# Block sums in small steps, a fast product begun one chunk later, and reloads on another queue

## The chip, the cores and the metric

The kernel runs on one core of one Trainium2 chip. Its metric is the device time of one execution in microseconds (us). Three runs took 912.3, 912.48 and 913.36 us; the median is 912.48 us. The profiled execution took 912.57 us, and 910.5 us of it lie between its first and its last instruction (the span).

## What is computed

Three stages follow one another: an attention over blocks, a gated feed-forward stage, and a second feed-forward stage with a residual. Only the last one is touched. Cut to what matters:

```
def _moe2_ref(x, g_ln, w_ch1, w_ch2):          # x: 4 x 576 x 512
    mu, var = mean(x), mean((x - mu) ** 2)      # over the last axis
    xn = (x - mu) / sqrt(var + 1e-06) * g_ln
    ch = maximum(xn @ w_ch1, 0.0) @ w_ch2       # w_ch1 512 x 2048, w_ch2 2048 x 512
    return x + ch
```

The weights arrive as 64-bit floats. Each is turned into a 32-bit float on the chip and then cut into a high and a low part, so that a product of two numbers is three matrix multiplications (high by high, low by high, high by low).

## The kernel before, in words

**Tiling.** The 2304 tokens are four groups of 512 (0, 1, 2, 3) and one of 256 (group 4, called `Z` in the code). The hidden dimension of 2048 is cut into eight chunks of 256 (`NC2` = 8, chunks 0 to 7). For each chunk every group goes through the first product (`em_c1`, 24 matmuls of 512 columns, written to PSUM tiles `ph`, five buffers), a ReLU on ScalarE and a split into high and low on VectorE (`h`), and then the second product (`em_c2`, six matmuls for each tile of 128 tokens, PSUM tiles `po`, three buffers), which VectorE adds to `acc` (line 794). The second product of a group is issued after the first product of the next group.

**The fast form.** For a pair of groups (`PAIRS`: 0 with 3, and 2 with 1) the first product can be made with seven block products in place of eight (`em_c1s`, 42 matmuls for the pair in place of 48). It needs four sums of blocks of the weights (`forms` inside `chunk_jobs`, tiles `ta` and `tb`) and four sums of blocks of the inputs (tiles `SF`, in the trace `s`). `sum_forms` makes the input sums: VectorE and GpSimd (POOL) add and subtract, ScalarE writes the high part of a sum, POOL the low part. Both pairs share the four `SF` tiles, so each sum is also stored to memory (`s_scr`) and reloaded (`load_form`, 1 MB each) whenever the other pair is next. `S3`, the fourth `SF` tile, holds half of group 3's inputs until the first sums replace them.

**When.** Chunk 0 uses the plain form for all groups. In it each group's inputs are also normalised (`ln_z`), transposed on TensorE (PE, line 632) and split (`ln_out`, line 641). The sums of the first pair are made during chunk 0, in four calls; chunk 1 uses the fast form for that pair, while the sums of the second pair are made, in four calls again; from chunk 2 on both pairs are fast.

**The weights of the next chunk** are converted by a pipeline of four jobs (`chunk_jobs`) of five stages: load by SP, two ScalarE operations ("above" and "below"), an integer subtraction on POOL (line 130) and a bit operation on VectorE (line 134), ScalarE's high part, POOL's low part. `Convert.step` moves every running job one stage on and starts one more. The scratch of "above" has one buffer, so a job's ScalarE operation waits for the bit operation of the job before it. The third job's VectorE stage also makes the four weight sums (line 605).

**Order.** All instructions stand in each engine's queue in the order in which the program issues them, and every engine, SP's queue included, works its queue off in order. So an operation that waits holds up everything behind it on its engine.

Of the kernel before, what the change touches and what calls it, by code (L numbers as in the profile page):

```python
# [32 lines left out]
def attention_moe_kernel(ctx, tc, raw_d, dup_d, raw0_d, dup0_d, v_d, v0_d, msk_d, mz_d, vec_d, eye_d, wk_d, wv_d, wr_d, wc1_d, wc2_d, out_d):  # L33
# [9 lines left out]
    def sub(eng, out, in0, in1):  # L43
        eng.tensor_tensor(out=out, in0=in0, in1=in1.bitcast(F32), op=ALU.subtract)  # L44
# [542 lines left out]
    def chunk_jobs(c):  # L587
        L, kept = [], []
        for k in (0, 2):
            w = wc1_d[128 * k:128 * k + 256, CF * c:CF * c + CF].rearrange("(a p) n -> p a n", a=2)  # L590
            L.append(load_split(w, lambda i, k=k: W[c % 2][0][i][:, k:k + 2], kept))
        for k in range(2):
            r0 = CF * c + 128 * k
            L += pieces(wc2_d[r0:r0 + 128], lambda i: W[c % 2][1][i], k, DM)
        if c:

            z = []

# [71 lines left out]
        x, k = XN[G, kk // 2][i]  # L670
        return x[:, kk - k]

    def sum_forms(pr):

        (g0, g1) = pr
        v, g = nc.vector, nc.gpsimd

        def block(G, h, k):
            return [x[:, k].bitcast(F32) for x in quarter(G, h)]

        def temp():
            return stg3.tile([128, 512], F32, name="a2")

        def split(i, k, z):
            act(SF[i][:, 0, k], z)
            sub(g, SF[i][:, 1, k], z, SF[i][:, 0, k])

        def both(a, b, op):
            z, t = temp(), temp()
            g.tensor_tensor(out=t, in0=a[1], in1=b[1], op=op)  # L690
            v.tensor_tensor(out=z, in0=a[0], in1=b[0], op=op)
            v.tensor_tensor(out=z, in0=z, in1=t, op=ALU.add)
            return z

        def third(k):
            split(2, k, both(block(g0, 0, k), block(g1, 0, k), ALU.subtract))

        def others(k):
            a, b = block(g0, 0, k), block(g0, 1, k)
            z = both(block(g1, 0, k), block(g1, 1, k), ALU.add)  # L700
            split(0, k, z)
            y = temp()
            v.tensor_tensor(out=y, in0=z, in1=a[0], op=ALU.subtract)
            v.tensor_tensor(out=y, in0=y, in1=a[1], op=ALU.subtract)
            split(1, k, y)
            x = temp()
            v.tensor_tensor(out=x, in0=b[0], in1=y, op=ALU.subtract)
            v.tensor_tensor(out=x, in0=x, in1=b[1], op=ALU.add)
            split(3, k, x)

        def store(*forms):
            for i in forms:
                nc.sync.dma_start(out=s_scr[PAIRS.index(pr), i], in_=SF[i].bitcast(F32))

        return [lambda: third(0), lambda: (third(1), store(2)), lambda: others(0), lambda: (others(1), store(0, 1, 3))]

    def load_form(pr, i):
        nc.gpsimd.dma_start(out=SF[i], in_=s_scr[PAIRS.index(pr), i])

    def em_c1s(c, pr, nxt, prev):  # L720

        g0, g1 = pr
        w1, tf = W[c % 2][0], TF[c]

        def bq(k, n):
            return [w[:, 2 * k:2 * k + 2, 128 * n:128 * n + 128] for w in w1]

        def prod(p, a, b, start=True):
            for x, (wi, xi) in enumerate(((0, 0), (1, 0), (0, 1))):
                for kk in range(2):  # L730
                    mm(p, b[wi][:, kk], a[xi][:, kk], start and kk == 0 and x == 0, kk == 1 and x == 2, skip_group_check=True)

        def s_(i):
            return [SF[i][:, 0], SF[i][:, 1]]

        def t_(i):
            return [t[:, i] for t in tf]

        def reload(i):
            if nxt is not None:  # L740
                load_form(nxt, i)

        def split(h1, m, p):
            act(h1[0][:, m], p, AF.Relu)
# [12 lines left out]
        split(u, 0, z)  # L757
        prod(d, s_(0), t_(0))
        reload(0)
        prod(e, s_(3), bq(1, 1))  # L760
        reload(3)
        prod(b, s_(1), t_(1), False)
        reload(1)
        z = temp()
        act(z, b)
        tt(out=z, in0=d, in1=z, op=ALU.add)
        tt(out=z, in0=e, in1=z, op=ALU.add)
        split(u, 1, z)
        prev()
        w = new_h1(c, g1)  # L770
        prod(b, s_(2), t_(2), False)
        reload(2)
        z = temp()
        act(z, b)
        tt(out=z, in0=d, in1=z, op=ALU.add)
        split(w, 1, z)
        em_c2(c, g0, (0, 1))
        prod(b, quarter(g1, 1), t_(3), False)
        split(w, 0, b)
        em_c2(c, g0, (2, 3))  # L780

    def em_c2(c, G, ts):
# [28 lines left out]
    with tc.manual_schedule():  # L811
# [280 lines left out]
            return [p.tile([128, 4, 2, 128], F32R, name=f"{name}{i}") for i in range(2)]  # L1092


        first = (0, 0, 0), (0, 0, 0), (0, 0, 1), (1, 1, 1), (2, 2, 2)

        def norms(x):

# [12 lines left out]
                    ln_z(i, eng=nc.gpsimd if x == 2 else nc.vector)  # L1111

        T["attention"] = True
        sums = []

        def some(n):
            for f in sums[:n]:
                f()
            del sums[:n]

        for x, G in enumerate(GORD):
            em_c1(0, G, lambda: norms(x))
            if x == 0:
                ln_scale(late[0], late[-1] + 1)
                conv = Convert(chunk_jobs(1))
            if x == 3:
                es_z.close()
                ft = opened(es_f, "ft", side=R)
                TF[1] = TF[2] = tf_tiles(ft, "ta")
            if x == 1:  # L1130
                sums += sum_forms(PAIRS[0])
            cs = first[x]
            conv.some(cs[0])
            if x:
                em_c2(0, GORD[x - 1], (0, 1))
            some(1)
            conv.some(cs[1])
            if x:
                em_c2(0, GORD[x - 1], (2, 3))
            some(1)  # L1140
            conv.some(cs[2])
        conv.all()
        todo = 0, GORD[-1]
        Z = GORD[2]
        for c in range(1, NC2):
            pr = PAIRS[::2 * (c % 2) - 1]
            conv = Convert(chunk_jobs(c + 1) if c + 1 < NC2 else [])
            c0, G0 = todo
            em_c1s(c, pr[0], pr[1] if c > 1 else None, lambda: em_c2(c0, G0, (0, 1, 2, 3)))
            if c == 1:  # L1150
                sums += sum_forms(PAIRS[1])
            else:
                conv.some(2)
            some(1)
            em_c1(c, Z)
            conv.some(1)
            some(1)
            em_c2(c, pr[0][1], (0, 1))
            some(1)
            conv.some(1)  # L1160
            em_c2(c, pr[0][1], (2, 3))
            some(1)
            conv.some(1)
            if c == 1:
                em_c1(c, pr[1][0])
                conv.some(2)
                em_c2(c, Z, (0, 1))
                conv.some(1)
                em_c1(c, pr[1][1])
                conv.some(2)  # L1170
                em_c2(c, pr[1][0], (0, 1))
                conv.some(2)
                em_c2(c, pr[1][0], (2, 3))
                conv.all()
                del XN[g3, 0], T["o1"]
                es_o.close()
                fo = opened(es_f, "ft1")
                tb = tf_tiles(fo, "tb")
                TF.update((k, TF[2] if k % 2 == 0 else tb) for k in range(3, NC2))
            else:  # L1180
                em_c1s(c, pr[1], None, lambda: em_c2(c, Z, (0, 1)))
                conv.all()
            todo = c, pr[1][1]
        em_c2(*todo, range(4))


# [64 lines left out]
```

## Time and profile before

| what | value |
|---|---|
| median of three runs | 912.48 us |
| profiled execution | 912.57 us |
| its span | 910.5 us |
| PE busy | 818.4 us (90%) |
| VectorE (DVE) busy | 582.2 us (64%) |
| ScalarE (ACT) busy | 429.6 us (47%) |
| POOL busy | 363.3 us (40%) |
| mean granted TensorE clock | 0.959 of full speed |

The busy share is a mean over the whole span. The three stages have different limits, so the last stage, from about 452 us on, has to be read by itself: when PE waits there, for how long, and what ended the wait. Chunk 1 begins at 532.34 us, chunk 2 at 602.10, chunk 3 at 651.5, chunk 7 at 853.8.

### The profile page before, as it was taken

How to read it: one execution, taken by the hardware profiler on the slowest of the kernel's cores; microseconds unless marked ns; L12 is line 12 of the kernel's file. 1: busy time of each engine (PE TensorE's matmuls, PEld its weight loads, DVE VectorE, ACT ScalarE, POOL GpSimd, SP SyncE). 2: the span in 40 equal slices, each digit the busy share in tenths (PEclk: the TensorE clock that was granted, in tenths of full speed). 3: DMA queues.
4: the chain of work that ended last, by engine and by line, in shares of the span. 5: the costliest groups of instructions: out<-in, count | busy, mean ns of one | idle time of the engine just before them, and what ended most of it. 6: DMA issues, size and time to landing. Idle time of an engine off the chain costs nothing.

```text
span 910.5 us, 10598 instructions
## 1 busy us (share of the span) xinstructions
PE 818.4 (90%) x3750; PEld 670.1 (74%) x3750; DVE 582.2 (64%) x1012; ACT 429.6 (47%) x736; POOL 363.3 (40%) x312
## 2 busy tenths in 40 slices
PE   4888988999999999999995779489999999999998
PEld 3656765668789899899874658368787878787786
DVE  6888899887854423434776556565666565666644
ACT  5876777887663343355441422333333342334311
POOL 6788579756751101101227333533313233233200
PEclk9998999999999999999998889789999999999999
DMA  8995478415301010005231601443250616152252
GB/s 226 322 322 167 145 228 262 138 47 196 115 24 70 24 47 35 35 21 188 85 112 53 224 24 70 185 148 129 79 179 21 231 46 231 47 190 87 81 197 116
DMA packets 44676, 117.20 MB, mean 129 GB/s; under 512 B 3984, under 2 KB 18448, under 8 KB 40528
## 3 DMA queue, kind: packets, MB, share of 16 engines
q1 hardware_dynamic: 35696, 69.00, 22.9%
q0 software_dynamic: 8496, 45.17, 14.7%
q10 hardware_dynamic: 432, 2.36, 0.6%
q8 instruction: 29, 0.48, 0.2%
q14 instruction: 23, 0.19, 0.1%
HBM read 96.33 MB, written 20.19 MB: 128 GB/s over the span
## 4 chain that ended last, share of the span: by engine, by line
PE 53%; DVE 22%; ACT 13%; POOL 5%; DMA 3%; issue 3%; SPq 0%; ACTq 0%; DVEq 0%; POOLq 0%
PE ph L348 15%; PE po L348 14%; PE p L348 13%; PE s L348 12%; DVE a L134 5%; ACT a L41 4%; DVE part L403 3%; ACT r L41 2%; POOL a L130 2%; ACT e L41 2%; DVE QK L436 1%; DVE mix L516 1%; ACT p L41 1%; DMA raw<-in_w_ch_dram 1%; POOL s L44 1%
## 5 line engine op out<-in xcount | busy, mean ns | idle before, releaser
L348 PE MATMUL po<-c,h 128*128 128x512 f32 x864 | 218.2, 405 | 24.2 <-DVE acc L794 15.7
L348 PEld LDWEIGHTS po<-c,h 128*128 128x128 f32 x864 | 167.3, 196 | 66.0 <-DVE acc L794 21.3
L794 DVE TENSOR_TENSOR acc<-po,acc 128x512 f32<-128x512 f32 x144 | 95.0, 685 | 28.5 <-PE po L348 27.5
L348 PE MATMUL ph<-x,c 128*128 128x512 f32 (+1 forms) x456 | 93.2, 351 | 16.7 <-DVE h L659 16.7
L348 PE MATMUL s<-x,wk 128*128 128x384 f32 x576 | 103.1, 338 | 0.6 <-POOL x L44 0.3
L348 PEld LDWEIGHTS s<-x,wk 128*128 128x128 f32 x576 | 101.3, 188 | 2.1 <-POOL x L44 1.1
L44 POOL TENSOR_TENSOR x<-mix,x 128x384 fp32r<-128x384 f32 x36 | 40.4, 1134 | 152.6 <-ACT x L41 147.2
L348 PE MATMUL p<-wv,k 128*128 128x512 f32 x432 | 99.7, 390 | 0.6 <-DVE k L44 0.6
L348 PE MATMUL p<-e,V 128*128 128x512 f32 (+4 forms) x320 | 99.1, 460 | 0.0
L348 PEld LDWEIGHTS ph<-x,c 128*128 128x128 f32 x456 | 75.2, 192 | 29.3 <-DVE h L659 17.2
L348 PEld LDWEIGHTS p<-wv,k 128*128 128x128 f32 x432 | 80.8, 188 | 17.6 <-DVE k L44 1.1
L348 PEld LDWEIGHTS p<-e,V 128*128 128x128 f32 x320 | 59.4, 199 | 36.4 <-issue 31.5
L130 POOL TENSOR_TENSOR a<-a,a 128x512 int32<-128x512 int32 x36 | 46.2, 1282 | 96.0 <-ACT a L41 95.9
L41 ACT ACTIVATE a<-raw,ce 128x512 int32<-128x512 int8 (+1 forms) x80 | 57.5, 751 | 55.8 <-DVE a L134 51.1
L44 POOL TENSOR_TENSOR c<-a,c 128x512 fp32r<-128x512 f32 x32 | 41.9, 1309 | 95.3 <-ACT c L41 95.3
L134 DVE SCALAR_TENSOR_TENSOR a<-raw,a 128x512 int32<-128x512 int32 x52 | 63.6, 1222 | 25.4 <-POOL a L130 24.0
L44 DVE TENSOR_TENSOR k<-a,k 128x768 fp32r<-128x768 f32 x24 | 23.7, 987 | 81.5 <-ACT a L41 81.5
L403 DVE TRANSPOSE_TENSOR_REDUCE part<-s 128x14 f32<-128x448 f32 (+4 forms) x160 | 65.0, 467 | 1.7 <-PE s L348 0.7
L41 ACT ACTIVATE u<-ph 128x512 f32<-128x512 f32 x39 | 23.1, 593 | 78.2 <-PE ph L348 74.4
L41 ACT ACTIVATE e<-s 128x1536 f32<-128x1536 f32 (+1 forms) x34 | 48.4, 1424 | 12.7 <-PE s L348 10.0
L348 PE MATMUL s<-wr,x 128*128 128x512 f32 x216 | 52.3, 404 | 1.9 <-DVE x L44 1.9
L41 ACT ACTIVATE a<-s 128x768 f32<-128x768 f32 x24 | 19.5, 812 | 67.6 <-PE s L348 63.4
(158 smaller groups left out, 1274.8 us busy)
## 6 DMA issues: line engine op xcount, KB each, us to landing
s<-s_scr POOLq DMA_DIRECT2D x24, 1024.0 KB, 7.5
kq<-in_dup_dram POOLq DMA_DIRECT2D x15, 1088.0 KB, 6.2
raw<-in_raw_dram SPq DMA_DIRECT2D x32, 288.0 KB, 4.2
s_scr<-s SPq DMA_DIRECT2D x8, 1024.0 KB, 4.3
raw<-in_w_ch_dram SPq DMA_DIRECT2D x16, 511.6 KB, 3.6
raw<-in_w_ch_dram SPq DMA_DIRECT2D x32, 255.6 KB, 3.6
V<-in_v_dram SPq DMA_DIRECT2D x16, 320.0 KB, 5.6
x_scr<-r SPq DMA_DIRECT2D x18, 256.0 KB, 2.0
```

The costliest lines, as they stand in the source:

```text
L41: nc.scalar.activation(out=out, in_=in_, func=func, **kw)
L44: eng.tensor_tensor(out=out, in0=in0, in1=in1.bitcast(F32), op=ALU.subtract)
L130: (nc.gpsimd if T.get("attention") else nc.vector).tensor_tensor(out=a1.bitcast(I32), in0=whole(a1), in1=whole(a2), op=ALU.subtract)
L134: stt(out=st["a2"].bitcast(I32), in0=w3, scalar=5, in1=st["a1"].bitcast(I32), op0=ALU.logical_shift_right, op1=ALU.bitwise_or)
L348: nc.tensor.matmul(out=out, lhsT=lhsT, rhs=rhs, start=start, stop=stop, **kw)
L403: red(out=pt[0:kp, b0:b0 + w // 32, j], in_=v3(s[0:kp, o:o + w]), axis=AX.X, op=ALU.max, apply_transpose=True)
L436: lambda x=x: tt(out=v3(dst)[:, x:x + 16], in0=m[:, x:x + 16].unsqueeze(2).to_broadcast([32, 16, 32]), in1=s[64:96, 512:544].unsqueeze(1). ...
L516: stt(out=m[:, o:o + w], in0=XT[b][:, kk, q0:q0 + w], scalar=omm[:, c + kk:c + kk + 1], in1=y[:, o:o + w], op0=ALU.mult, op1=ALU.add)
L794: tt(out=acc[i], in0=p, in1=acc[i], op=ALU.add)
```

## The change

- **The first pair turns fast in chunk 2, the second in chunk 3**, one chunk later than before. Chunk 1 becomes plain for all five groups, chunk 2 plain for the second pair.
- **The input sums are made in nine steps for each pair**, the first pair's in chunk 1, the second's in chunk 2. A new function `tick` is called between pieces of PE work (after each half of a first product, after each two tiles of a second). Each call does one step of the sums, if any are left, and one step of the weights' conversion, after a count of calls to wait (8 in chunk 1, 7 in chunk 2).
- **The sums' scratch** is a pool of four tiles of its own; it lay in `stg3` with the conversion's. Of VectorE's 32 operations on the sums of both pairs, four become POOL operations (a subtraction in place, in `second`).
- **From chunk 3 on** the conversion's steps stand at ten ticks spread over the chunk. Before, two steps stood after the first fast pair, three around group `Z`, the rest at the chunk's end.
- **The reloads** of `SF` are issued by SP (20 of them). Before, POOL issued 24.

Core of the diff:

```
-        if c:
+        if c > 1:                                   # weight sums only from chunk 2
...
-    def sum_forms(pr):
+    def sum_forms(pr, pool):
...
+        def first(k):
+            both(block(g1, 0, k), block(g1, 1, k), ALU.add)      # POOL t, DVE z
+        def second(k):
+            z, a = st.pop("z"), block(g0, 0, k)
+            op(v, z, z, st.pop("t"), ALU.add)
+            split(0, k, z)
+            op(v, temp("y"), z, a[0])
+            op(g, st["y"], st["y"], a[1])
+        def third(k):
+            y = st.pop("y")
+            split(1, k, y)
+            op(v, temp("x"), block(g0, 1, k)[0], y)
+        def fourth(k):
+            x = st.pop("x")
+            op(v, x, x, block(g0, 1, k)[1], ALU.add)
+            split(3, k, x)
+        def fifth(k):
+            both(block(g0, 0, k), block(g1, 0, k), ALU.subtract)
+        def sixth(k):
+            z = st.pop("z")
+            op(v, z, z, st.pop("t"), ALU.add)
+            split(2, k, z)
...
-        nc.gpsimd.dma_start(out=SF[i], in_=s_scr[PAIRS.index(pr), i])
+        nc.sync.dma_start(out=SF[i].bitcast(F32), in_=s_scr[PAIRS.index(pr), i])
...
-        first = (0, 0, 0), (0, 0, 0), (0, 0, 1), (1, 1, 1), (2, 2, 2)
+        first = (0, 0, 0), (0, 0, 1), (0, 0, 0), (0, 1, 1), (1, 1, 2)
...
+        def tick():
+            if work["sums"]:
+                work["sums"].pop(0)()
+                if not work["sums"]:
+                    work["es"].close()
+                    open_forms(*work["next"])
+            if work["wait"]:
+                work["wait"] -= 1
+            else:
+                conv.step()
+        def group(c, G, todo):
+            c0, G0 = todo
+            em_c1(c, G, tick)
+            tick()
+            em_c2(c0, G0, (0, 1))
+            if G0 != Z:
+                tick()
+                em_c2(c0, G0, (2, 3))
+            tick()
+            return c, G
```

**Where instructions stand now.** First VectorE's queue in chunk 0, before (rows of before; `h` is the split after a first product, `x` and `o` the transposed inputs, `a` scratch, `acc` the additions after a second product). The stretch lies between the second product of group 3 and the first product of group 2:

```order
L794 TENSOR_TENSOR acc_3722<-po,acc_3722 128x512
L794 TENSOR_TENSOR acc_3723<-po,acc_3723 128x512
L691 TENSOR_TENSOR a_4237<-s_3740,x_3738 128x512
L692 TENSOR_TENSOR a_4237<-a_4237,a_4238 128x512
L703 TENSOR_TENSOR a_4244<-a_4237,x_3712 128x512
L704 TENSOR_TENSOR a_4244<-a_4244,x_3713 128x512
L707 TENSOR_TENSOR a_4249<-x_3712,a_4244 128x512
L708 TENSOR_TENSOR a_4249<-a_4249,x_3713 128x512
L659 SCALAR_TENSOR_TENSOR h_4261<-ph,h_4260 128x512
L641 SCALAR_TENSOR_TENSOR o_3925<-ph,vec,o_3925 128x512 x2
```

The same stretch in the changed kernel:

```order
L818 TENSOR_TENSOR acc_3722<-po,acc_3722 128x512
L818 TENSOR_TENSOR acc_3723<-po,acc_3723 128x512
L659 SCALAR_TENSOR_TENSOR h_4209<-ph,h_4208 128x512
L641 SCALAR_TENSOR_TENSOR o_3925<-ph,vec,o_3925 128x512 x2
L641 SCALAR_TENSOR_TENSOR x_3744<-ph,vec,x_3743 128x512 x2
L659 SCALAR_TENSOR_TENSOR h_4209<-ph,h_4208 128x512
```

The sums that stood ahead of the split `h` have left chunk 0.

Next VectorE's queue at the end of chunk 2 in the changed kernel, in the plain first product of group 1 and the second product of group 2 (`t` is the sums' scratch, L134 the bit operation of the conversion, `raw` the weight sums):

```order
L683 TENSOR_TENSOR t<-t,x_3742 128x512
L683 TENSOR_TENSOR t<-x_3741,o_3925 128x512
L134 SCALAR_TENSOR_TENSOR a_5072<-raw_5047,a_5070 128x512
L659 SCALAR_TENSOR_TENSOR h_5110<-ph,h_5109 128x512
L683 TENSOR_TENSOR t<-t 128x512
L683 TENSOR_TENSOR t<-x_3741,o_3925 128x512
L134 SCALAR_TENSOR_TENSOR a_5105<-raw_5074,a_5103 128x512
L659 SCALAR_TENSOR_TENSOR h_5110<-ph,h_5109 128x512
L683 TENSOR_TENSOR t<-t 128x512
L134 SCALAR_TENSOR_TENSOR a_5138<-raw_5107,a_5136 128x512
L605 TENSOR_TENSOR raw_5171<-a_5072 128x256
L818 TENSOR_TENSOR acc_3716<-po,acc_3716 128x512
```

Steps of the sums, steps of the conversion and PE's own splits alternate there, and the first addition to `acc` of group 2 stands behind all of them.

Last SP's queue at the beginning of chunk 4, in the changed kernel (`s` are the `SF` tiles, `raw` the weights to convert):

```order
L739 DMA s_3916<-s_scr 128x2048
L739 DMA s_3740<-s_scr 128x2048
L739 DMA s_3917<-s_scr 128x2048
L99 DMA raw_5642<-in_w_ch_dram 128x2045 x2
L739 DMA s_3918<-s_scr 128x2048
L99 DMA raw_5695<-in_w_ch_dram 128x2045 x2
```

In the kernel before, only the loads of weights stood here, and the reloads in POOL's queue.

## Rows read from the trace of the kernel before

**Rows 1.** Stretches of the trace by chunk: us, PE, PEld, DVE, ACT, POOL, clock, DMA.

```profile
452.25:532.34 80.09, 55.70 (x262) 46.11 (x261) 54.05 (x77) 27.80 (x48) 37.60 (x25) 0.85 0.35 122
532.34:602.10 69.76, 53.84 (x224) 42.42 (x222) 44.58 (x56) 20.57 (x34) 29.12 (x22) 0.85 0.26 94
602.10:651.61 49.51, 47.46 (x218) 38.91 (x217) 28.87 (x43) 17.38 (x28) 11.42 (x12) 1.00 0.32 113
651.61:853.80 202.19, 193.97 (x866) 158.25 (x865) 123.71 (x176) 71.53 (x116) 58.82 (x53) 0.97 0.36 125
```

**Rows 2.** Timeline of PE in chunk 0: start, us, instructions, idle before.

```profile
472.79 1.91 PE L632 MATMUL ph<-eye,z 128*128 128x128 f32 x16
...
504.66 4.93 PE L348 MATMUL ph<-x,c 128*128 128x512 f32 x12 [14.62 <-DVE h L659]
...
529.61 2.93 PE L348 MATMUL po<-c,h 128*128 128x512 f32 x6 [7.70 <-DVE acc L794]
```

**Rows 3.** Timeline of POOL in chunk 0.

```profile
477.34 8.74 POOL L625 TENSOR_SCALAR z<-acc,mv,rsd 128x512 f32<-128x512 f32 x4
```

**Rows 4.** Chain that ended last, in order of time: start, us, what.

```profile
505.71 5.48 DMA raw<-in_w_ch_dram
...
546.79 2.75 PE po L348 x12
```

**Rows 5.** Timeline of PE at the end of chunk 1.

```profile
585.57 2.99 PE L348 MATMUL po<-c,h 128*128 128x512 f32 x6 [7.85 <-ACT h L41]
595.21 7.05 PE L348 MATMUL po<-c,h 128*128 128x512 f32 x18 [6.64 <-DVE acc L794]
```

**Rows 6.** Timeline of all engines, one link of the input sums in chunk 1.

```profile
559.59 0.69 DVE L692 TENSOR_TENSOR a<-a,a 128x512 f32<-128x512 f32 x1 [1.18 <-POOL a L690]
...
560.31 0.63 ACT L41 ACTIVATE s<-a 128x512 fp32r<-128x512 f32 x1 [3.28 <-DVE a L692]
...
561.02 1.29 POOL L44 TENSOR_TENSOR s<-a,s 128x512 fp32r<-128x512 f32 x1 [1.47 <-ACT s L41]
...
562.26 1.74 POOL L690 TENSOR_TENSOR a<-o,x 128x512 f32<-128x512 f32 x1
...
564.04 0.69 DVE L692 TENSOR_TENSOR a<-a,a 128x512 f32<-128x512 f32 x1 [1.18 <-POOL a L690]
```

**Rows 7.** Timeline of all engines, links of the conversion in chunk 4.

```profile
726.21 5.66 PE L348 MATMUL po<-c,h 128*128 128x512 f32 x24
...
727.17 0.68 DVE L134 SCALAR_TENSOR_TENSOR a<-raw,a 128x512 int32<-128x512 int32 x1
...
730.62 1.31 POOL L44 TENSOR_TENSOR c<-a,c 128x512 fp32r<-128x512 f32 x1
730.70 1.78 DVE L134 SCALAR_TENSOR_TENSOR a<-raw,a 128x512 int32<-128x512 int32 x1 [0.85 <-POOL a L130]
...
732.51 1.41 ACT L41 ACTIVATE a<-raw,ce 128x512 int32<-128x512 int8 x2 [2.70 <-DVE a L134]
...
737.82 0.88 DVE L605 TENSOR_TENSOR raw<-a,raw 128x256 f32<-128x256 f32 x2
```

**Rows 8.** Timeline of PE in chunk 4.

```profile
702.36 2.92 PE L348 MATMUL ph<-x,c 128*128 128x512 f32 x12
...
723.35 3.02 PE L348 MATMUL ph<-x,c 128*128 128x256 f32 x24
...
788.72 2.92 PE L348 MATMUL ph<-s,tb 128*128 128x512 f32 x6 [2.02 <-ACT u L41]
```

**Rows 9.** Waits of PE from 605 to 905 us: total, times, longest.

```profile
PE ph L348 <- ACT u L41: 9.8, 5, 2.0
```

**Rows 10.** Timeline of ACT in chunk 4.

```profile
718.03 0.63 ACT L41 ACTIVATE h<-u 128x512 fp32r<-128x512 f32 x1 [0.76 <-DVE u L775]
```

**Rows 11.** Timeline of DVE in chunk 4.

```profile
721.43 0.69 DVE L745 SCALAR_TENSOR_TENSOR h<-ph,h 128x512 fp32r<-128x512 f32 x1 [0.84 <-ACT h L41]
```

**Rows 12.** DMA from 704 to 718 us: GB/s in 40 slices of 0.35 us.

```profile
GB/s 0 0 0 0 29 129 245 263 356 327 310 304 356 409 386 345 375 398 492 374 421 351 421 374 398 468 398 398 445 421 421 421 445 398 421 375 164 94 23 23
```

More of the change, by code (lines that the diff above doesn't have):

```diff
@@ L671, in xn, with op, temp @@
         return x[:, kk - k]
-    def sum_forms(pr):
+    def sum_forms(pr, pool):
         (g0, g1) = pr
         v, g = nc.vector, nc.gpsimd
+        st = {}
         def block(G, h, k):
             return [x[:, k].bitcast(F32) for x in quarter(G, h)]
-        def temp():
-            return stg3.tile([128, 512], F32, name="a2")
+        def op(eng, out, in0, in1, op=ALU.subtract):
+            eng.tensor_tensor(out=out, in0=in0, in1=in1, op=op)
+        def temp(n):
+            st[n] = pool.tile([128, 512], F32, name="t")
+            return st[n]
         def split(i, k, z):
@@ L686, in split @@
             sub(g, SF[i][:, 1, k], z, SF[i][:, 0, k])
[L688 to L693, printed above, removed]
-        def third(k):
[L696 to L704, printed above, removed]
+            if k:
+                nc.sync.dma_start(out=s_scr[PAIRS.index(pr), i], in_=SF[i].bitcast(F32))
@@ L705, in others, with both @@
+        def both(a, b, how):
+            op(g, temp("t"), a[1], b[1], how)
+            op(v, temp("z"), a[0], b[0], how)
+        def first(k):
[6 more added lines that the diff above has]
+            op(g, st["y"], st["y"], a[1])
+        def third(k):
+            y = st.pop("y")
             split(1, k, y)
-            x = temp()
@@ L707, in others @@
-            v.tensor_tensor(out=x, in0=b[0], in1=y, op=ALU.subtract)
-            v.tensor_tensor(out=x, in0=x, in1=b[1], op=ALU.add)
+            op(v, temp("x"), block(g0, 1, k)[0], y)
+        def fourth(k):
+            x = st.pop("x")
+            op(v, x, x, block(g0, 1, k)[1], ALU.add)
             split(3, k, x)
[L711 to L715, printed above, removed]
+        def fifth(k):
+            both(block(g0, 0, k), block(g1, 0, k), ALU.subtract)
@@ new lines, in sixth @@
+        def sixth(k):
+            z = st.pop("z")
+            op(v, z, z, st.pop("t"), ALU.add)
+            split(2, k, z)
+        if pr == PAIRS[0]:
+            return [
+                lambda: fifth(0), lambda: (sixth(0), fifth(1)), lambda: (sixth(1), first(0)), lambda: second(0), lambda: third(0),
+                lambda: (fourth(0), first(1)), lambda: second(1), lambda: third(1), lambda: fourth(1),
+            ]
+        return [
+            lambda: first(0), lambda: second(0), lambda: third(0), lambda: (fourth(0), first(1)), lambda: second(1), lambda: third(1),
+            lambda: (fourth(1), fifth(0)), lambda: (sixth(0), fifth(1)), lambda: sixth(1),
+        ]
@@ L717, in load_form, with em_c1s @@
     def load_form(pr, i):
[L718 to L720 removed]
+        nc.sync.dma_start(out=SF[i].bitcast(F32), in_=s_scr[PAIRS.index(pr), i])
+    def em_c1s(c, pr, nxt, prev, tick):
         g0, g1 = pr
@@ L1113, in attention_moe_kernel @@
         T["attention"] = True
[L1114 to L1119, printed above, removed]
+        Z = GORD[2]
         for x, G in enumerate(GORD):
@@ L1125, in attention_moe_kernel @@
                 conv = Convert(chunk_jobs(1))
[L1126 to L1131, printed above, removed]
             cs = first[x]
@@ L1135, in attention_moe_kernel @@
                 em_c2(0, GORD[x - 1], (0, 1))
-            some(1)
             conv.some(cs[1])
@@ L1139, in attention_moe_kernel, with open_sums, open_forms @@
                 em_c2(0, GORD[x - 1], (2, 3))
-            some(1)
             conv.some(cs[2])
-        conv.all()
+        es_z.close()
         todo = 0, GORD[-1]
-        Z = GORD[2]
-        for c in range(1, NC2):
-            pr = PAIRS[::2 * (c % 2) - 1]
+        work = {"sums": [], "wait": 0}
+        def open_sums(pr):
+            work["es"] = ExitStack()
+            tz = opened(work["es"], "tz", 4, side=R)
+            work["sums"] = sum_forms(pr, tz)
+        def open_forms(*cc):
+            work["ef"] = es_f if len(cc) > 1 else ExitStack()
+            ft = opened(work["ef"], "ft", side=R)
+            ta = tf_tiles(ft, "ta")
+            for c in cc:
+                TF[c] = ta
@@ new lines, in tick @@
+        def tick():
[11 more added lines that the diff above has]
+            em_c1(c, G, tick)
+            tick()
+            em_c2(c0, G0, (0, 1))
+            if G0 != Z:
+                tick()
+                em_c2(c0, G0, (2, 3))
+            tick()
+            return c, G
@@ L1147, in attention_moe_kernel @@
+        for c in range(1, NC2):
+            pr = PAIRS[::1 - 2 * (c % 2)]
+            if c == 1:
+                conv.all()
+                work["wait"], work["next"] = 8, (2,)
+                open_sums(PAIRS[0])
+            elif c == 2:
+                work["wait"], work["next"] = 7, range(3, NC2, 2)
             conv = Convert(chunk_jobs(c + 1) if c + 1 < NC2 else [])
-            c0, G0 = todo
-            em_c1s(c, pr[0], pr[1] if c > 1 else None, lambda: em_c2(c0, G0, (0, 1, 2, 3)))
@@ L1150, in attention_moe_kernel @@
             if c == 1:
-                sums += sum_forms(PAIRS[1])
-            else:
[L1153 to L1182, printed above, removed]
@@ L1183, in attention_moe_kernel @@
-            todo = c, pr[1][1]
+                for G in (0, 3, Z, 2, 1):
+                    todo = group(c, G, todo)
+            else:
+                c0, G0 = todo
+                em_c1s(c, pr[0], pr[1] if c > 2 else None, lambda: em_c2(c0, G0, (0, 1, 2, 3)), tick)
+                if c == 2:
+                    del TF[2]
+                    work["ef"].close()
+                    open_sums(PAIRS[1])
+                todo = group(c, Z, (c, pr[0][1]))
+                if c == 2:
+                    for G in pr[1]:
+                        todo = group(c, G, todo)
+                    conv.all()
+                    del XN[g3, 0], T["o1"]
+                    es_o.close()
+                    fo = opened(es_f, "fb")
+                    tb = tf_tiles(fo, "tb")
+                    for k in range(4, NC2, 2):
+                        TF[k] = tb
+                else:
+                    em_c1s(c, pr[1], None, lambda: em_c2(c, Z, (0, 1)), tick)
+                    todo = c, pr[1][1]
@@ L1184, in attention_moe_kernel @@
+            conv.all()
         em_c2(*todo, range(4))
```

## The prediction

> **What bounds the kernel now.** I read the stretches by chunk first [rows 1], then PE's timeline for its waits [rows 2, 5, 8, 9], and then the engine that each wait names [rows 3, 6, 7]. PE is the bound of the last stage while nothing stops it. Twelve matmuls of 512 columns follow one another in 2.75 us [rows 4], 0.229 us each, and a group `Z` product of 24 narrow ones takes 2.85 us, from 723.35 to 726.21 [rows 7, 8]. A chunk has 108 matmuls in its second products. With both pairs fast it has 84 in its first products, so it could take 192 x 0.229 + 2.85 = 46.8 us; with one fast pair 48.2, with none 49.6. The change makes one chunk fast later for each pair, which is 12 matmuls or 2.75 us more; they are in these figures.
>
> Against this, chunk 1 takes 69.8 us, chunk 2 49.5, and chunks 3 to 6 202.2 for 4 x 46.8 = 187.2 [rows 1]. In chunk 0 PE waits 14.62 us for VectorE's split and 7.70 us for its `acc` addition [rows 2]; at the end of chunk 1 7.85 and 6.64 us [rows 5]. VectorE isn't slow at these splits: sums and conversion steps stand ahead of them in its queue, and each waits for POOL or ScalarE. After such a wait PE is slow as well. Twelve matmuls took 4.93 us after the 14.62 us [rows 2], and the granted clock was 0.85 over chunks 0 and 1 [rows 1].
>
> **Chunk 0: 29.5 us less.** The sums leave it. The transposes for group 2 end at 474.7 [rows 2]. What PE has left until chunk 1 is 12 narrow matmuls (1.43 us), 24 (5.5), 12 (2.75), 16 transposes (1.9), 12 and 12 (5.5), 24 and 24 (11.0): 28.1 us, so 502.8 in place of 532.34. Could POOL's four normalisations of 8.74 us [rows 3] hold this up? They stood behind a split of the sums; now they can start near 473.3, when the first transposes free a buffer, and end at 482.1, and the transposes that need them come at 484.4. The conversion's last steps are the tighter cover: POOL's low part of the second half of the first weights ends near 503.5, and PE wants it at 504.1. If that cover goes, each link below costs about 4.5 us once.
>
> **Chunk 1: 64.5 us for 69.8, 5.3 less.** PE alone would need 49.6, but the nine steps form a ring through three engines. One link (VectorE adds, ScalarE copies, POOL splits, POOL forms the next half) takes 4.45 us, from 559.59 to 564.04 [rows 6], while ticks come every 2.75 us. For each half k the sums 0, 1 and 3 need: add 0.75, copy 0.65, split 1.35, POOL's new subtraction 1.3, VectorE's 0.7 beside the copy, add 0.7 and the place of `acc` ahead of it 1.4, copy 0.75, split 1.35, next half 1.3, about 9.5 us. So two links of 4.45 and two of 9.5: 28 us. They begin at 6.8 after the chunk's start, behind the last conversion steps, and with PE's own splits between end at 36. The first load of weights stands behind the store of the last sum in SP's queue and lands 5.5 us after its issue, like the 5.48 of [rows 4]: 42. Then four conversion links: ScalarE pair 1.41, subtraction 1.3, bit operation 0.68 or 1.78 [rows 7], plus a ReLU and split between, about 4.3 us each, to 59.4. The additions of `Z` stand behind the last bit operation, PE needs their buffers for four tiles of group 2, and chunk 2 begins at 64.5. Bounds: 49.6 if everything hides, 75 if every paired sum waits as below.
>
> **Chunk 2: 75.5 us for 49.5, 26.0 more.** Up to group `Z` nothing is added: 21.0 us as from 702.36 to 723.35 [rows 8]. From `Z` on the ring runs again: six sum steps have reached POOL at 20.3 us, but the first load, behind the first store, is issued at 17.4 and lands at 22.9. ScalarE's pair waits for it and holds up the next copy, so POOL's split comes at 25.0. From here steps of both kinds alternate with PE's splits, and nothing overlaps: split, next half and subtraction 3.9; bit operation 0.75; pair 1.45; ReLU, split and add 2.05; copy 0.7; POOL three operations 3.95; bit 0.75; pair 1.45; ReLU, split, add 2.05; copy 0.7; POOL three 3.95; bit 1.8 with a low part beside it; four weight sums 1.65 [rows 7]; first `acc` addition 0.7. Together 25.9 us, so 50.9. PE can be three tiles of group 2 ahead, no more. Then one tile, 1.4 us, and the slow clock, 2.2 by 4.93 less 2.75 [rows 2, 4]: 54.5. Bounds: 27.6 (all hidden) and 62.
>
> **Chunks 3 to 6: 0.8 us more.** Now PE waits 2 us in each, at the second fast pair [rows 9], with the clock 3.7 (14.9 us over four). This wait goes, because the conversion is past its middle there. What is late next is the fourth tile after group `Z`. PE reaches it 28.0 us into the chunk (726.21 and three tiles [rows 7]). The first bit operation stands behind a split that ends at 19.8 [rows 11]; from there bit 0.7, pair 1.4, subtraction 1.4, bit 0.9, pair 1.45, ReLU and subtraction 1.35, bit 1.8, weight sums 1.65 and addition 0.7 make 31.2. A wait of 3.2 us and some 0.7 for the clock: 3.9 for 3.7, times four. Bounds for a chunk: 1 and 7. The 0.53 to 0.64 us that POOL spent on each reload were beside PE's work and are worth nothing; SP has no other work that PE waits for, apart from the loads (second rival).
>
> One thing is counted low on purpose. The bit operation took 0.68 us alone, and 1.78 when POOL's low part began 0.08 us ahead of it [rows 7]; I count these 1.1 us at that operation and once at the start of the sums, since most paired sums are queued behind different releases (fourth rival).
>
> **The sum.** -29.5 - 5.3 + 26.0 + 0.8 = -8.0. The profiled execution took 912.57 us, 2.1 us of it outside the span and unchanged, and lies 0.1 above the median. Forecast: 904.5 us.
>
> **Rivals.** (1) *The steps run beside PE as their spacing of 2.75 us suggests.* For it: ScalarE is busy 20.6 of 69.8 us in chunk 1, POOL 29.1 [rows 1], so there is room. Against it: the links are latency, not load. With a third of the ring showing, chunk 1 would take 54 and chunk 2 57: 912.6 - 29.5 - 15.8 + 7.5 = 875, and a little less in chunks 3 to 6: 873.
>
> (2) *Slower: the reloads hold up the weights.* In SP's queue three reloads stand ahead of the first load. They wait for PE until 6.9 us into a chunk, 3.15 MB, and the load's 0.5 MB comes behind. At some 0.4 MB/us [rows 12] from 5 us on the load lands near 14.5; ScalarE wants it at 16.3, where its queue is free (718.66 less 702.36 [rows 8, 10]). Each microsecond beyond that goes into the four waits; from 18.3 on the 8 us are gone. If it lands at 21, chunks 3 to 6 cost 19 us more: 923. Against it speaks the margin of 1.8 us. The Trainium skill (DMA: Bandwidth & Descriptors, "Issuing engines are not separate DMA queues") says that transfers of all queues share the same DMA engines; by that the data would land at about the same time from either queue. No row here shows a reload from SP.
>
> (3) *Chunk 0 doesn't get what it should:* the wait for VectorE becomes one for POOL's normalisations or for the conversion's low part, and half of the 29.5 us stays: 919.
>
> (4) *Paired sums stop each other.* The steps put a sum on VectorE and one on POOL side by side, some ten times in each of chunks 1 and 2. If each costs the 1.1 us of [rows 7], both chunks become 11 us longer: 926. Against it: the additions of [rows 6] took 0.69 us, though POOL had finished only just before. The Trainium skill (SBUF — State Buffer, "SBUF: two separate sides") says that a VectorE operation with two inputs in SBUF and a GpSimd operation lock each other out for a whole instruction, which would give this rival its cause; the pair of [rows 7] agrees with it.
>
> **How the numbers follow.** Forecast 0.48 (its own range 896 to 912), rival 1 0.18, rival 2 0.18, rival 3 0.10, rival 4 0.06. The range of 8 in 10 leaves out half of rival 1 below, and the far parts of rivals 2 and 4 above: 882 to 922. A measurement of this kernel can tell 0.2%, 1.8 us. Faster: 0.18, 0.44 of the forecast's 0.48, and 0.03 from a mild rival 2 or 3: 0.65. Same: 0.03 of the forecast and 0.06 of these: 0.09. Slower: the remaining 0.26.
>
> **What would show it.** Chunk 1 should begin near 503, with no wait of PE over 1 us between 475 and it. Chunk 2 should begin near 567, and PE's longest wait of the run, over 20 us, should stand at the fourth tile of group 2's second product in chunk 2, ended by an `acc` addition. In chunks 3 to 6 the wait for ScalarE's `u` should be gone and one of about 3 us for an `acc` addition should have come. Wrong would be: a wait at chunk 2's end below 10 us (rival 1), ScalarE's conversion waiting for a DMA in chunks 3 to 6 (rival 2), chunk 1 beginning after 512 (rival 3).

## The result, and the profile after

The changed kernel takes 920.72 us (median of four runs, 920.21 to 922.99) against 912.92 for the kernel before (912.3 to 913.49): a ratio of 1.009, 95% interval 1.0071 to 1.011. It is slower by 0.9%, where the prediction said 0.9% faster. The profiled execution took 920.21 us, with a span of 918.4 us.

The stretches of the last stage in the changed kernel, in the columns of [rows 1]. The lines are chunk 0, chunk 1, chunk 2, chunks 3 to 6, chunk 7:

```profile
451.20:501.28 50.08, 50.08 (x262) 42.58 (x260) 32.35 (x54) 19.60 (x35) 12.89 (x8) 1.00 0.29 95
501.28:569.63 68.35, 54.63 (x229) 42.85 (x228) 38.72 (x53) 20.88 (x35) 36.86 (x28) 0.95 0.27 97
569.63:642.69 73.06, 49.88 (x223) 40.82 (x222) 35.33 (x54) 20.38 (x34) 27.17 (x22) 0.84 0.24 87
642.69:861.33 218.64, 197.63 (x866) 161.01 (x864) 122.31 (x177) 72.35 (x117) 55.08 (x38) 0.94 0.32 116
861.33:918.40 57.07, 52.80 (x241) 43.11 (x239) 27.00 (x41) 9.34 (x16) 0.00 (x0) 1.00 0.41 157
```

| term | before, us | after, us | difference | predicted |
|---|---|---|---|---|
| start of the last stage | 452.25 | 451.20 | -1.1 | 0 |
| chunk 0 | 80.09 | 50.08 | -30.0 | -29.5 |
| chunk 1 | 69.76 | 68.35 | -1.4 | -5.3 |
| chunk 2 | 49.51 | 73.06 | +23.6 | +26.0 |
| chunks 3 to 6 | 202.19 | 218.64 | +16.4 | +0.8 |
| chunk 7 | 56.70 | 57.07 | +0.4 | 0 |
| sum (the span) | 910.5 | 918.4 | +7.9 | -8.0 |

Chunk 3 was predicted to begin at 642.8 us (502.8 + 64.5 + 75.5) and begins at 642.69. The miss is in chunks 3 to 6, 15.6 us. That chunk 3 begins where it was forecast is in part luck: chunk 1 was put 3.9 us too low, and chunk 2 (2.4 us too high), chunk 0 (0.5) and the start of the stage (1.1) make that up.

PE's timeline of the changed kernel, at the end of chunk 2 and at the same place of chunk 4 (start, us, instructions, idle before and what ended it):

```profile
612.62 4.28 PE L348 MATMUL po<-c,h 128*128 128x512 f32 x18
639.97 2.93 PE L348 MATMUL po<-c,h 128*128 128x512 f32 x6 [23.07 <-DVE acc L818]
...
721.51 4.29 PE L348 MATMUL po<-c,h 128*128 128x512 f32 x18
730.42 2.92 PE L348 MATMUL po<-c,h 128*128 128x512 f32 x6 [4.62 <-DVE acc L818]
733.14 3.79 PE L348 MATMUL ph<-x,c 128*128 128x512 f32 x12
```

After 18 matmuls, three tiles, PE stands still until VectorE has added a tile to `acc`: 23.07 us in chunk 2, and 5.56, 4.62, 4.89 and 5.55 us in chunks 3 to 6. The wait for ScalarE's `u` of [rows 9] is gone. Next, the weight loads of the conversion's first two jobs in chunk 4, which begins at 697.68 us; each job has a pair of loads. First SP's queue, then ScalarE's.

```profile
702.00 3.04 SPq L739 DMA_DIRECT2D s<-s_scr  x3
705.15 0.84 SPq L99 DMA_DIRECT2D raw<-in_w_ch_dram  x2
711.96 0.33 SPq L739 DMA_DIRECT2D s<-s_scr  x1
712.38 0.85 SPq L99 DMA_DIRECT2D raw<-in_w_ch_dram  x2
```

```profile
714.45 1.42 ACT L41 ACTIVATE a<-raw,ce 128x512 int32<-128x512 int8 x2 [0.50 <-DMA raw<-in_w_ch_dram]
...
718.98 1.42 ACT L41 ACTIVATE a<-raw,ce 128x512 int32<-128x512 int8 x2 [2.29 <-DMA raw<-in_w_ch_dram]
```

The first pair of loads stands behind three reloads, the second behind the fourth, which waits for PE until 711.96. The second pair lands at 718.98, 21.3 us into the chunk, 6.6 us after its issue. What follows in the same chunk, on VectorE and then on POOL (its low part):

```profile
721.80 1.78 DVE L134 SCALAR_TENSOR_TENSOR a<-raw,a 128x512 int32<-128x512 int32 x1 [0.68 <-POOL a L130]
...
726.40 1.76 DVE L134 SCALAR_TENSOR_TENSOR a<-raw,a 128x512 int32<-128x512 int32 x1 [0.67 <-POOL a L130]
...
729.68 1.28 DVE L818 TENSOR_TENSOR acc<-po,acc 128x512 f32<-128x512 f32 x2
```

```profile
721.71 1.32 POOL L44 TENSOR_TENSOR c<-a,c 128x512 fp32r<-128x512 f32 x1
```

The second bit operation, begun 0.09 us after POOL's low part, takes 1.78 us, and the addition that frees a buffer for PE begins at 729.68. The granted clock around this wait, by stretch (the columns of [rows 1]):

```profile
726.00:730.42 4.42, 0.00 (x1) 0.01 (x1) 3.95 (x7) 2.14 (x4) 2.15 (x3) 0.75 0.10 40
730.42:733.40 2.98, 2.98 (x7) 2.40 (x8) 2.73 (x3) 1.25 (x2) 2.98 (x3) 0.50 0.00 0
733.40:737.00 3.60, 3.60 (x14) 2.83 (x14) 0.78 (x2) 0.84 (x2) 3.10 (x2) 0.78 0.00 0
737.00:741.00 4.00, 4.00 (x19) 3.34 (x18) 1.38 (x2) 0.63 (x1) 0.00 (x0) 1.00 0.00 0
```

After the wait PE is at 0.50, 1.2 GHz, for about 3 us and is back at full speed within 7 us. The tile of six takes 2.72 us from start to start instead of 1.37, the twelve after it 3.63 instead of 2.75: 2.2 us beside the wait itself.

### The profile page after: what moved, and what is told of

The parts are those of the page before. It is cut to its first block, busy times and chain, and to the rows that moved or that the text cites. A ratio compares the mean times of both kernels' runs of the same rounds, so it can differ in the third digit from the quotient of the medians.

```text
span 918.4 us, 10591 instructions
## 1 busy us (share of the span) xinstructions
PE 815.3 (89%) x3762; PEld 669.9 (73%) x3762; DVE 557.6 (61%) x996; ACT 424.9 (46%) x729; POOL 353.1 (38%) x291
## 4 chain that ended last, share of the span: by engine, by line
PE 48%; DVE 21%; ACT 11%; issue 6%; DMA 6%; POOL 6%; SPq 0%; ACTq 0%; DVEq 0%; POOLq 0%
PE ph L348 14%; PE po L348 11%; PE s L348 11%; PE p L348 11%; DVE a L134 5%; DVE part L403 4%; DMA raw<-in_w_ch_dram 4%; POOL a L130 3%; ACT r L41 2%; ACT a L41 2%; ACT e L41 2%; DVE QK L436 2%; POOL t L683 2%; DVE mix L516 1%; POOL s L44 1%
## 5 line engine op out<-in xcount | busy, mean ns | idle before, releaser
L348 PE MATMUL ph<-x,c 128*128 128x512 f32 (+1 forms) x504 | 107.6, 358 | 0.3 <-POOL c L44 0.3
L348 PEld LDWEIGHTS ph<-x,c 128*128 128x128 f32 x504 | 85.7, 195 | 15.6 <-POOL c L44 0.8
L348 PE MATMUL p<-e,V 128*128 128x512 f32 (+4 forms) x320 | 94.3, 443 | 0.0
L134 DVE SCALAR_TENSOR_TENSOR a<-raw,a 128x512 int32<-128x512 int32 x52 | 61.0, 1174 | 38.9 <-POOL a L130 37.5
L348 PEld LDWEIGHTS p<-e,V 128*128 128x128 f32 x320 | 57.5, 194 | 33.5 <-issue 28.4
L41 ACT ACTIVATE u<-ph 128x512 f32<-128x512 f32 x33 | 19.7, 598 | 98.1 <-PE ph L348 94.2
L348 PE MATMUL s<-QK 128*128 128x512 f32 (+4 forms) x160 | 32.6, 337 | 22.9 <-DVE QK L436 22.6
```

Source lines behind the costliest of these rows:

```text
L41: nc.scalar.activation(out=out, in_=in_, func=func, **kw)
L134: stt(out=st["a2"].bitcast(I32), in0=w3, scalar=5, in1=st["a1"].bitcast(I32), op0=ALU.logical_shift_right, op1=ALU.bitwise_or)
L348: nc.tensor.matmul(out=out, lhsT=lhsT, rhs=rhs, start=start, stop=stop, **kw)
```

## The experiments

Two causes were open for the loss in chunks 3 to 6: the conversion's new places put too much ahead of the addition that PE waits for, or the reloads in SP's queue make its weights late (rival 2). The kernel before ran beside each experiment; ratios are to it. "The four waits" are those of PE at the fourth tile after group `Z` in chunks 3 to 6.

**1. The reloads back on POOL's queue.**

```
-        nc.sync.dma_start(out=SF[i].bitcast(F32), in_=s_scr[PAIRS.index(pr), i])
+        nc.gpsimd.dma_start(out=SF[i], in_=s_scr[PAIRS.index(pr), i])
```

> The changed kernel with one part undone: the reloads of the input sums go through POOL's queue again. The changed kernel took 920.7 us and waits 4.6 to 5.6 us at the fourth tile in each of chunks 3 to 6. Theory A (place: the conversion's middle steps stand ahead of the first acc additions after group Z, and that alone makes the wait): only the 0.5 to 2.3 us for which ScalarE waits for the first two loads go; the waits become 3.5 to 4.5 us and the time 914 to 918 us. Theory B (queue: the reloads in SP's queue delay the weights): the waits fall to 2 us or less and the time is about 905 us.

Measured: 912.53 us, ratio 0.9998 (0.9984 to 1.0012). That lies between what the two theories asked for. The four waits are 2.80, 2.85, 2.80 and 2.78 us, a load lands 3.1 us (median) after its issue, and chunks 3 to 6 take 208.8 us: 9.8 of the 16.4 us are gone. PE's timeline of this kernel in chunk 4 shows a part of the rest, in the same columns:

```profile
728.04 2.93 PE L348 MATMUL po<-c,h 128*128 128x512 f32 x6 [2.85 <-DVE acc L818]
730.77 4.52 PE L348 MATMUL ph<-x,c 128*128 128x512 f32 x12
```

The wait is 0.35 us below the 3.2 that I had predicted, yet 18 matmuls after it take 7.1 us instead of 4.1.

**2. The conversion's steps in their places of before, in chunks 3 to 6; reloads still on SP.**

```
...
-                todo = group(c, Z, (c, pr[0][1]))
+                    conv.some(2)
+                    em_c1(c, Z)
+                    conv.some(1)
+                    em_c2(c, pr[0][1], (0, 1))
+                    conv.some(1)
...
```

> The changed kernel with another part undone: in chunks 3 to 6 the conversion's steps stand where they stood before (two after the first fast pair, three around group Z, the rest at the chunk's end); the reloads stay with SP. Theory A (place): the waits at the fourth tile go, the 2 us waits for ScalarE's u come back, chunks 3 to 6 take 202 us as before and the time is 902 to 907 us. Theory B (queue): the loads are late here too, the waits for u grow beyond 4 us, and the time is over 912 us.

Measured: 904.48 us, ratio 0.9924 (0.9901 to 0.9947), as expected. Chunks 3 to 6 take 204.4 us. The waits for `u` are back (2.13, 1.97, 1.91, 1.96), and the four waits are gone. So the loss in chunks 3 to 6 needs the new places: with the old ones, loads behind the reloads cost little (204.4 us for the 202.2 of the kernel before). The rest of the change, the sums' new order and the later turn to the fast form, is a gain by itself.

**3. One more step of the conversion at the start of each of chunks 3 to 6.**

```
+                if c > 2:
+                    conv.step()
                 em_c1s(c, pr[0], ...)
```

> The changed kernel with one step of the conversion more at the beginning of chunks 3 to 6, so that every step stands one tick earlier and the first load ahead of the reloads. Theory A (place): the bit operation of the third job and the weight sums are done before PE reaches the fourth tile, no wait over 1 us is left in chunks 3 to 6, these take 188 to 192 us and the time is 890 to 896 us. Theory B (queue): the second load still lands behind three reloads and ScalarE waits for it; the waits stay at 3 us or more and the time is 908 us or more.

Measured: 917.33 us, ratio 1.0068 (1.0042 to 1.0095); the four waits 4.15, 4.41, 4.16 and 4.67. Theory A missed. The numbers of theory B came, but not by its cause, as ScalarE's second pair in chunk 4 shows, which begins 17.6 us into the chunk and waited for VectorE, not for its load. VectorE's timeline behind it tells what happened:

```profile
716.02 1.41 ACT L41 ACTIVATE a<-raw,ce 128x512 int32<-128x512 int8 x2 [1.36 <-DVE a L134]
```

```profile
726.18 0.88 DVE L605 TENSOR_TENSOR raw<-a,raw 128x256 f32<-128x256 f32 x2
727.42 0.42 DVE L659 SCALAR_TENSOR_TENSOR h<-ph,h 128x256 fp32r<-128x256 f32 x1 [0.36 <-ACT h L41]
728.49 1.75 DVE L134 SCALAR_TENSOR_TENSOR a<-raw,a 128x512 int32<-128x512 int32 x1 [0.65 <-POOL a L130]
730.16 1.87 DVE L818 TENSOR_TENSOR acc<-po,acc 128x512 f32<-128x512 f32 x3
```

The third job's bit operation and the weight sums are done by 727.06. But the fourth job moved forward by a step as well, and its bit operation now stands ahead of the addition.

**4. Four buffers for `po` and four for `ph` from chunk 3 on, instead of three and five.**

```
...
+            if c == 3:
+                es_b.close()
+                ph = es_f.enter_context(tc.tile_pool(name="ph", bufs=4, space=PSUM))
+                po = es_f.enter_context(tc.tile_pool(name="po", bufs=4, space=PSUM))
```

> The changed kernel with PSUM cut differently from chunk 3 on: four buffers for the second product and four for the first, in place of three and five. Nothing is moved in any queue. Theory A (place): the fourth tile has a buffer of its own, PE runs on into the next fast pair and the waits of 5 us go: 890 to 900 us, unless the fast form then waits for its fifth buffer. Theory B (queue): says nothing else here, since it too makes PE wait at this tile; it would expect the lateness to come up again at the second fast pair, 910 us or more.

Measured: 904.33 us, ratio 0.9915 (0.9888 to 0.9943); chunks 3 to 6 take 205.2 us. The four waits vanish, so the buffers were what PE waited for. But the late chain comes out one place further on: PE now waits 2.86, 2.10, 2.89 and 2.32 us for ScalarE's `u`. Theory B had named that place. The time lies between the two expectations, 4 us above A's and 6 below B's.

**5. SP keeps the reloads; the loads of the first two jobs stand ahead of them.**

```
+                if c > 2:
+                    for j in conv.jobs[:2]:
+                        j[0]()                 # the load
+                        j[0] = lambda: None
                 em_c1s(c, pr[0], ...)
```

> The changed kernel; in chunks 3 to 6 only the loads of the first two conversion jobs stand earlier in SP's queue, ahead of the reloads; these stay with SP and all other steps where they are. With the reloads in POOL's queue the waits at the fourth tile were 2.8 us and the time 912.5 us. Theory C (order in SP's queue: the loads stand behind reloads that wait for PE): the waits fall to 2.7 to 3.2 us and the time is 911 to 914 us, as with POOL. Theory D (the transfers themselves: reloads issued by SP are in the way of the weights whatever the order): the waits stay at 4.5 us or more and the time is over 917 us.

Measured: 910.61 us, ratio 0.9983 (0.9967 to 0.9998). SP's queue, then VectorE's, then POOL's low part, for chunk 4, which begins at 694.81 here:

```profile
676.39 3.06 SPq L99 DMA_DIRECT2D raw<-in_w_ch_dram  x4
699.12 10.27 SPq L739 DMA_DIRECT2D s<-s_scr  x4
```

```profile
718.14 0.68 DVE L134 SCALAR_TENSOR_TENSOR a<-raw,a 128x512 int32<-128x512 int32 x1
...
724.99 1.28 DVE L818 TENSOR_TENSOR acc<-po,acc 128x512 f32<-128x512 f32 x2
```

```profile
718.37 1.62 POOL L44 TENSOR_TENSOR c<-a,c 128x512 fp32r<-128x512 f32 x1 [0.42 <-ACT c L41]
```

The four loads go out in chunk 3 and land after 3.2 us. The second bit operation now begins 0.23 us ahead of POOL's low part and takes 0.68 us; it is the low part that gets longer, 1.62 us instead of 1.32. The addition comes 30.2 us into the chunk instead of 32.0, the four waits are 2.80, 2.81, 2.80 and 2.79, and chunks 3 to 6 take 208.7 us, as in experiment 1. So the queue's owner doesn't matter. What matters is that the reloads stand ahead of the loads. This run doesn't tell whether the late issue harms or the megabytes in front, since it takes both away.

**6. Reloads of a sixteenth of the size, the queue's order unchanged.**

```
-        nc.sync.dma_start(out=SF[i].bitcast(F32), ...)
+        nc.sync.dma_start(out=SF[i][:, :, :, 0:32].bitcast(F32), ...)
```

> The changed kernel, but each of the 20 reloads on SP's queue moves only a sixteenth of its tile (64 KB in place of 1 MB; the other fifteen sixteenths of the block sums are left out, so its output differs). The order of SP's queue and the waits for TensorE stay. Late issue alone: the loads are still issued some 7.5 and 14.7 us into a chunk, so if the hold-up in the queue is what counts, the second pair still comes too late: the four waits at the fourth tile stay at 4.6 to 5.6 us and the time at 918 to 922. Late issue together with the shared transfer: the loads now land in 3.2 to 3.7 us instead of a median of 6.6, the second pair at about 18.2 us into the chunk, before ScalarE's queue is free for it (20.4); the four waits fall to 2.8 us, chunks 3 to 6 take 208 to 210, and the time is 909 to 912.

Measured: 910.39 us, ratio 0.9982 (0.9966 to 0.9998). SP's queue in chunk 4, which begins at 695.59 here, then the times from issue to landing of the weight loads in 640 to 865 us:

```profile
699.90 3.24 SPq L739 DMA_DIRECT2D s<-s_scr  x3
703.25 1.02 SPq L99 DMA_DIRECT2D raw<-in_w_ch_dram  x2
709.86 0.53 SPq L739 DMA_DIRECT2D s<-s_scr  x1
710.49 1.04 SPq L99 DMA_DIRECT2D raw<-in_w_ch_dram  x2
...
DMA to landing us min/median/max: 3.0/3.3/4.8
```

The issue is as late as before, 7.7 and 14.9 us into the chunk, but the loads land in 3.3 us. The four waits are 2.80, 2.89, 2.80 and 3.03. So here the late issue alone is harmless; the load has to share the way with the reloads in front of it as well.

**7. The second pair of loads ahead of the fourth reload.**

```
...
         prod(b, s_(2), t_(2), False)
+        T.pop("ahead", lambda: None)()         # load of the second job
         reload(2)
```

> The changed kernel, with the second pair of weight loads one place earlier in SP's queue in chunks 3 to 6: ahead of the fourth reload, right behind the first pair. If the fourth reload, which waits for TensorE until 14.3 us into a chunk, is what makes the second pair late, both pairs are issued by 9 us and the second lands near 18 to 19 us; ScalarE's second pair then starts at about 20.4 instead of 21.3, the second bit operation falls clear of POOL's low part (0.7 us instead of 1.8), the waits are 2.8 to 3.3 us and the time 910 to 914. If it is the three first reloads, 3 MB, that slow both pairs, landing moves little (20 us or later) and the time stays at 917 to 921.

Measured: 915.5 us, ratio 1.0035 (1.0014 to 1.0056), between the two cases. All four loads are now issued behind three reloads, by 706.2, 10.0 us into chunk 4, and take 8.7 us (median) to land. ScalarE's second pair begins at 717.07, 20.8 us into the chunk, 0.5 us earlier than in the changed kernel, and no longer waits for its load. In chunk 4 the second bit operation still takes 1.78 us; the four waits are 3.08, 4.16, 2.80 and 4.59.

**8. Reloads on POOL, two steps at each chunk's start, none inside group `Z`.**

```
...
+                if c > 2:
+                    conv.some(2)
...
+                    em_c1(c, Z)
+                    em_c2(c, pr[0][1], (0, 1))
+                    tick()
+                    em_c2(c, pr[0][1], (2, 3))
+                    tick()
```

> The changed kernel with the reloads in POOL's queue; in chunks 3 to 6 two steps of the conversion stand at the chunk's beginning and none within group Z, so that the weight sums stand ahead of group Z and the fourth job's bit operation behind the first two acc additions after it. One step earlier alone did not help (917.3 us), and its rows showed the fourth job's bit operation ahead of these additions. Theory A (what counts is which VectorE steps stand ahead of the first acc addition after group Z): no wait over 0.7 us in chunks 3 to 6, 188 to 192 us for the four, time 889 to 895 us. If A is wrong and the conversion as a whole is too long to hide beside PE, a wait of 2 us or more shows at another place and the time stays over 900 us.

Measured: 896.89 us, ratio 0.9828 (0.9812 to 0.9845). Chunks 3 to 6 in this kernel, in the columns of [rows 1]:

```profile
643.97:837.98 194.01, 189.72 (x866) 155.02 (x864) 124.19 (x177) 71.73 (x117) 63.00 (x54) 1.00 0.37 130
```

The time is 2 us above the range expected, because waits of 0.7 to 1.1 us and of 0.28 us remain in each chunk. The granted clock is 1.00. The chunks take 194.0 us; 187.2 of that is PE's own work and 4.3 its waits, which leaves 0.6 us per chunk.

**9. Chunk 2's conversion beside the first fast pair, ahead of the sums.** Two steps at the chunk's start, no calls to wait; the weight sums' high and low parts are written after the last input sum.

```
...
-                work["wait"], work["next"] = 7, range(3, NC2, 2)
+                work["wait"], work["next"] = 0, range(3, NC2, 2)
...
+                if c == 2:
+                    conv.some(2)
```

> The changed kernel; in chunk 2 the conversion's steps stand two at the chunk's beginning and one at each tick from the first on, beside the first fast pair; only the two operations that write the weight sums stay behind the last input sum. In the changed kernel conversion and sums alternate on a ring at the chunk's end and PE waits 23.1 us at the fourth tile. Theory (the ring is one chain of 26 us because both kinds of steps share it): the wait falls to 3 to 9 us, chunk 2 from 73.1 to 53 to 58 us, and the time from 920.7 to 902 to 906 us. Rival (the sums alone fill the stretch, or the conversion holds up the fast pair's own splits): the wait or new waits stay at 15 us in sum and the time is over 912 us.

Measured: 907.69 us, ratio 0.9954 (0.9936 to 0.9972). The end of chunk 2 on PE:

```profile
627.03 2.93 PE L348 MATMUL po<-c,h 128*128 128x512 f32 x6 [5.49 <-DVE acc L821]
```

The wait falls from 23.07 to 5.49 us and the chunk from 73.1 to 59.3, 1.3 us more than the most expected; the time is 1.7 us above its range. So steps of both kinds alternating in the queues made most of that wait, as the prediction had it. The rest is probably the ring of the sums by itself: between 605 and 630 us VectorE's sums still wait five times for POOL's, 7.6 us in all. No run takes that out.

**10. Experiments 8 and 9 together.**

> The two kernels with two steps early in chunks 3 to 6 (reloads in POOL's queue) and with the conversion early in chunk 2, put together. Both theories right: 920.7 less 28 less 17, 873 to 879 us. If the two gains stand for the same wait, about 890 us.

Measured: 885.55 us, ratio 0.9701 (0.9686 to 0.9716), 3% faster than the kernel before and the fastest version here. Chunk 2 and chunks 3 to 6:

```profile
571.50:630.79 59.29, 50.42 (x223) 40.63 (x222) 38.39 (x54) 19.20 (x32) 29.14 (x23) 0.97 0.20 76
630.79:826.77 195.98, 191.04 (x866) 155.74 (x865) 123.99 (x176) 71.22 (x116) 61.94 (x53) 0.99 0.38 133
```

It misses its expectation by about 7 us. That was the sum of two expected gains, 28 and 17 us; experiments 8 and 9 gave 24 and 13, and the two together give 35. The 5.49 us wait in chunk 2 stays.

## Why the prediction was wrong

**Chunk 0: right.** 30.0 us less for 29.5. No wait of PE is left in it, so rival 3 is out.

**Chunk 1: 3.9 us too low, with the waits in other places.** The waits of PE in it sum to 13.7 us, near the 14.9 that 64.5 us implied, but that is in part luck: they stand at seven places of 0.3 to 2.7 us, spread over the chunk and not at its end, and I had counted no slow matmuls beside them. Its granted clock is 0.95. No experiment was made on this chunk.

**Chunk 2: right.** 73.06 us for 75.5, with the longest wait of the run, 23.07 us, at the tile and with the releaser that were named. Experiment 9 shows the cause. So rivals 1 and 4, with chunk 2 at 57 us or 11 us longer, are out.

**Chunks 3 to 6: the step that failed.** I predicted 50.7 us per chunk, 46.8 + a wait of 3.2 + 0.7 for the clock. Measured is 54.7: 46.8 + a wait of 5.2 + 2.7 beside it. Both terms were mis-sized, by about 8 us each over four chunks.

*The wait: 5.2 for 3.2 us.* The chain was the right one, and with the weights there in time the waits are 2.8 us (experiments 1, 5 and 6). What failed is the step that took the weights as landed. Rival 2 had this mechanism, and the measured 920.72 us is near its 923. Its sign came as well: in chunks 3 to 6 ScalarE's conversion waited for a DMA eight times, 13.8 us in all. I weighed only the first pair of loads: estimated at 14.5 us into the chunk, it came at 16.8, 0.5 late. The second pair, behind the fourth reload, I didn't follow at all, though the order of SP's queue shows it there. It came at 21.3. That moved the second bit operation 0.8 us back and behind the start of POOL's low part, where it takes 1.78 instead of 0.68 us. Together these are the 1.8 us between 30.2 (experiment 5) and 32.0.

The rule weighed there (the Trainium skill, DMA: Bandwidth & Descriptors, "Issuing engines are not separate DMA queues") says that transfers from all queues share the same DMA engines. The runs agree in part: a reload lands in about the same time from POOL's queue (median 7.6 us in the kernel before) as from SP's (6.8), and only with small reloads does a load behind them land fast (3.3 for 6.6 us). But I drew from it that the loads would land at about the same time either way. They did not, since from POOL's queue the reloads no longer stood ahead of the loads: these went out in the chunk before.

For the 1.78 us, the Trainium skill (SBUF — State Buffer, "SBUF: two separate sides") says that a VectorE operation with two inputs in SBUF and a GpSimd operation that reads SBUF lock each other out for a whole instruction, and that the one that starts second waits. The traces agree: where POOL's low part began 0.09 us ahead, the bit operation took 1.78 us, and where the bit operation began 0.23 us ahead (experiment 5), it took 0.68 and the low part 1.62.

*The rest beside the wait: 2.7 for 0.7 us.* This was an error of working, not of knowledge. The rows of before already had the price: their four waits of 1.96 us went with 14.9 us over 187.2, so 1.8 us each beside the wait. I took these 3.7 us out with the old wait and put 0.7 in with a longer new one. With 1.8 the sum would have been -3.6 instead of -8.0 us, 909 us, and with the measured waits of 5.2 us 917. Nor is all of it the clock. Chunk 4 of the kernel before, in the columns of [rows 1]:

```profile
702.36:751.77 49.41, 47.35 (x217) 38.76 (x216) 30.87 (x44) 17.91 (x29) 14.76 (x14) 1.00 0.36 128
```

At the full clock it takes 46.8 + a wait of 1.95 + 0.7 us, and experiment 8, also at 1.00, leaves 0.6 us per chunk. So the 46.8 us is itself some 0.6 us too low. The slow matmuls after a wait are the other 2 us in the changed kernel; they are gone in experiment 8.

**The sum.** Experiment 2, without the new places, measures 904.48 us, the forecast's 904.5. That is in part luck: the forecast had the new places in it, at 0.8 us, and chunks 3 to 6 take 204.4 us there for its 203.0.

## What to carry to other kernels

A transfer that waits for a compute engine in an in-order queue can delay every load behind it, by its wait and by its bytes; here the wait alone cost nothing (experiment 6), the two together did. Follow every load in that queue, not only the first, and put the loads ahead. Moving steps earlier in smaller pieces helps only if the operation that frees the bound engine's buffer doesn't get another step in front of it: count what stands ahead of that operation. Price a wait of the bound engine with the slow stretch after it, and take the same price for the wait that goes and the one that comes.

## What the runs showed of the hardware

A wait's length doesn't decide whether PE slows down after it. In the kernel of experiment 6 PE waited 2.80 us in chunk 3 and 2.80 us in chunk 5, each time at the same tile. The stretches behind these two waits, in the columns of [rows 1]:

```profile
676.12:679.00 2.88, 2.88 (x12) 2.36 (x13) 2.62 (x3) 1.15 (x2) 2.88 (x3) 1.00 0.00 0
...
776.74:779.60 2.86, 2.86 (x7) 2.28 (x8) 2.60 (x3) 1.14 (x2) 2.86 (x3) 0.51 0.03 6
```

Twelve matmuls at the full clock in the first, seven at half of it (1.2 GHz) in the second. The kernel before has the same pair: 2.92 us for six matmuls after a wait of 2.02 [rows 8], and on PE in chunk 4

```profile
739.29 1.65 PE L348 MATMUL ph<-s,ta 128*128 128x512 f32 x6 [1.95 <-ACT u L41]
```

So such a wait costs about 1.3 us more or not, plus what the next twelve lose. What decides stays open.
